# Probability spreads issued in pieces of two copies, and copies of product banks to G on ScalarE or VectorE

## The chip, the cores and the metric

The kernel runs on one core of a Trainium2 chip. A core has five engines with queues of their own: TensorE (PE in the profile; its weight loads are PEld), VectorE (DVE), ScalarE (ACT), GpSimd (POOL) and SyncE (SP, which here issues DMAs only). Each engine takes its instructions in the order in which the program lists them, and waits for others by semaphores. Matrix products land in PSUM banks of 128 x 512 fp32, which only TensorE, ScalarE and VectorE reach in this kernel; everything else lies in SBUF or in DRAM.

The metric is the device time of one execution in microseconds, smaller is better.

## The reference

Sparse attention over 8 batches and 8 heads, then a feed-forward layer with a gated activation:

```python
def _attn_ref(q, k, v):                      # (8, 8, 576, 64) fp32
    ...
    rel = pos[:, None] - pos[None, :]
    mask_local = (rel >= 0) & (rel < 32)
    mask_strided = (rel >= 0) & (pos[None, :] % 32 == pos[:, None] % 32)
    # heads 0 to 3 use mask_local, heads 4 to 7 mask_strided
    ...
    attn = np.exp(scores)
    attn = attn / (np.sum(attn, axis=-1, keepdims=True) + 1e-09)
    return np.matmul(attn, v)

def _moe_ref(x, w_in, w_out):                # x: (4608, 512), d_ff = 2048
    h = x @ w_in
    g = h * np.clip(h + 3.0, 0.0, 6.0) / 6.0
    return g @ w_out
```

## The kernel before

**Attention** goes by pairs of heads (`pair(g)`, four pairs to a batch, two local and two strided). For each head of a pair the scores lie in a tile `e`. VectorE, ScalarE and GpSimd turn them into probabilities (mask, maximum, exponential, sum, division). For batches 2 to 7 VectorE then transposes them in place in 32 x 32 blocks (`flip`, L691), and ScalarE copies the blocks to their places in a larger tile `at`, which is zero elsewhere (`spread`, L693 to L701): a local head takes six copies of 32 partitions (L701, tile `atloc`), a strided head four (L698, tile `atstr`). All copies of one head are one operation of the plan. In a strided pair GpSimd then sets a column of `e` again (`again`, L704), and TensorE multiplies `at` with the values (`values`, L725; matmuls in L400 and L736).

**The feed-forward layer** works on tiles of 512 tokens. Every fp32 operand is split into a high and a low part, and every product takes three matmuls (high x high, high x low, low x high). Batches 0, 1 and 2 go through plain tiles (`ffn`). Batches 3 and 4, then 5 and 6, then 7 with the remaining rows of all batches, go in three double tiles, which use Strassen's scheme: seven products P1 to P7 in place of eight for a 2 x 2 block of hidden units (`product`, matmuls in L1130 to L1132, six for each product). The first double tile is `super_tile`, the two others are `fast_tile`; `form` prepares their operands (`B_B`, `B_T`, splits in L1060 and L1064, differences in L1070).

The products of a step share two PSUM banks, `("ph", 0)` and `("ph", 1)`. P1, P6, P7 and P4 use the one, P2, P5 and P3 the other. Some products begin a bank anew, others add to what the bank holds, since the scheme needs running sums. After a product its bank has to be read before the next product may write there. It is read in one of three ways:

- `copied` (L1135): the bank is copied into a tile `G` (or `r`) in SBUF by ScalarE, L1137. Three of the seven products of a step are read so: 72 copies in the whole kernel, 24 in each double tile.
- `added` (L1140): VectorE adds the bank to what `G` holds, L1142. The gate follows on it: a Relu by ScalarE (L777) and a product by VectorE (L780).
- for P4 the gate reads the bank itself (L1334 and L1338 in `fast_tile`).

In `fast_tile` the second layer is a product with seven terms as well (matmuls in L1453 to L1455, read by VectorE in L1465 to L1471); its operands are sums of the G tiles (L1402 to L1411) and their splits (L1364 and L1368).

**The order of the work** comes from a planner in the kernel, `Plan`. Each call of `op` gives an engine (or several, in a dictionary with the time for each), an estimated time in us, what it reads and writes, and a due time. `emit` walks forward in time like a simulator. For each engine it looks for the operation that can start first, and among equals for the one due first; then it takes the engine whose first operation starts earliest. The engines are looked at in the order in which their names first occur in the plan, and a later one is taken only if it is strictly earlier:

```python
for e, r in ready.items():
    ...
    if first is not None and (best is None or first[0] < best[0]):
        best = (first[0], e, first[2])
```

GpSimd and VectorE occur ahead of ScalarE. An operation that follows another on the same engine is available 0.02 us after it (L154). When all is placed, the instructions are issued in the order of the planned starts; on the chip each engine keeps that order, whatever the real times are.

The function that holds L693 to L706 is `pair`; `copied` stands in L1135 to L1138.

Of the kernel before, what the change touches and what calls it, by code (L numbers as in the profile page):

```python
# [28 lines left out]
PAD = 32  # L29
# [31 lines left out]
class Plan:  # L61
# [12 lines left out]
    def op(self, engine, us, fn, reads=(), writes=(), due=0.0, room=0.0, mode="", after=0.0, take=None, give=None, early=0.0):  # L74
        n = len(self.ops)
        before = set()
        for k in reads:
            if k in self.wrote:
                before.add(self.wrote[k])
            self.used.setdefault(k, []).append(n)  # L80
        for k in writes:
            if k in self.wrote:
                before.add(self.wrote[k])
            before.update(self.used.pop(k, ()))
            self.wrote[k] = n
        before.discard(n)
        how = engine if isinstance(engine, dict) else {engine: us}
        self.ops.append((how, fn, before, due, room, mode, after, take, give, early))
        return n
# [85 lines left out]
def attention_ffn(ctx: ExitStack, tc, q, k, v, w_in, w_out, out):  # L175
    nc = tc.nc
# [21 lines left out]
    op = plan.op  # L198
    tiles = {}
# [121 lines left out]
    def slot(early):  # L321

        return Slot([("acc", i) for i in range(4 if early == 2 else 2)] + [("s", i) for i in range(2)] if early else [("s", i) for i in range(2)])

    def psum(key, name):
        return new(pp, key.key if isinstance(key, Slot) else key, [P, TOK], F32, name)
# [17 lines left out]
    def timing(g):  # L344
        b = g // NPAIR
        if not b:
            return T0 - 6.0 * (NPAIR - g)
        return wanted[b] - 6.0 - (NPAIR - 1 - g % NPAIR) * (wanted[b] - opens[b]) / NPAIR
# [20 lines left out]
    def upright(ps, half, c0, data):  # L369

        rows = data.shape[0]
        nc.tensor.matmul(ps[D * half:D * half + D, c0:c0 + rows], data, tiles["ident",][:rows, :rows], start=True, stop=True)
# [68 lines left out]
    def pair(g):  # L441
# [3 lines left out]
        loc = h0 < H // 2  # L445
        nm = f"{b}_{c}"
        early = (b == 0) + (g == 0)
        due = timing(g)
# [30 lines left out]
        for x in "qk":  # L479
# [6 lines left out]
            if early:  # L486
# [32 lines left out]
                for h in range(2):  # L519
                    op({"ACT": 0.45, "DVE": 0.4} if loc else {"ACT": 0.65, "DVE": 0.65}, 0, partial(evac, h=h), reads=[tb[h]],  # L520
                       writes=[tkey[x]] if h == 0 else [(tkey[x], 1)], give=tb[h], due=due - 19)
# [49 lines left out]
        ekeys = [("el" if loc else "es", j) for j in range(2)]  # L571
        akeys = [("at64" if first else "atl" if loc else "at", j) for j in range(2)]
        stkey = ("st", g % 2)
        nblk = NQB if loc else 8
        n = QB if loc else P
# [4 lines left out]
        def e_whole(j):  # L580
            t = tiles["e", j]
            return t[:QB, :NQB * WIN].rearrange("p (u x) -> p u x", x=WIN) if loc else \
                t[:, NQB * WIN:NQB * WIN + 8 * PAD].rearrange("p (u x) -> p u x", x=PAD)
# [30 lines left out]
        for j in range(2):  # L614
# [5 lines left out]
            def keep(j=j):  # L620
# [17 lines left out]
               writes=[ek, st], give=banks[j], due=sd + 0.5)  # L638
# [40 lines left out]
        for j in range(2):  # L679
            def turn(j=j):  # L680
                at, e = tiles[akeys[j]], e_whole(j)
                for a in range(n // PAD):
                    rows = slice(PAD * a, PAD * a + PAD)
                    if not loc:
                        nc.vector.transpose(at[rows, :, rows], e[rows])
                        continue
                    for h in range(2):
                        nc.vector.transpose(at[PAD * (a + h):PAD * (a + h) + PAD, :, rows], e[rows, :, PAD * h:PAD * h + PAD])
            if b >= 2:
                def flip(j=j):  # L690
                    nc.vector.transpose(e_whole(j)[:, :, :2 * PAD if loc else PAD], e_whole(j)[:, :, :2 * PAD if loc else PAD])  # L691

                def spread(j=j):  # L693
                    at, e = tiles[akeys[j]], e_whole(j)
                    for a in range(n // PAD):
                        rows = slice(PAD * a, PAD * a + PAD)
                        if not loc:
                            nc.scalar.copy(at[rows, :, rows], e[rows])  # L698
                            continue
                        for h in range(2):  # L700
                            nc.scalar.copy(at[PAD * (a + h):PAD * (a + h) + PAD, :, rows], e[rows, :, PAD * h:PAD * h + PAD])  # L701

                def again(j=j):
                    nc.gpsimd.memset(e_whole(j)[:, :, NPOS:NPOS + 1], 1.0e-9)  # L704
                op("DVE", 0.55 if loc else 0.4, flip, writes=[ekeys[j]], due=due - 2 + j)
                op("ACT", 6 * 0.31 if loc else 4 * 0.36, spread, reads=[ekeys[j]], writes=[akeys[j]], due=due - 1.9 + j)  # L706
                if not loc:
                    op("POOL", 0.15, again, writes=[ekeys[j]], due=due - 1.8 + j)
                continue
            if not first:  # L710
                op("DVE", 6 * 0.37 if loc else 4 * 0.435, turn, reads=[ekeys[j]], writes=[akeys[j]], due=due - 2 + j)
                continue
            tb = slot(early)

            def stand(j=j, tb=tb):
                ps = psum(tb, f"pe{nm}{j}")
                for i in range(NQB):
                    upright(ps, i // 3, i % 3 * QB, e_whole(j)[:, i, :w])

            def copy(j=j, tb=tb):  # L720
                nc.scalar.copy(tiles["at64"][:, j], tiles[tb.key][:, :3 * QB])
            op("PE", 0.7 * slow, stand, reads=[("ident",), ekeys[j]], writes=[tb], take=tb, due=due - 1002 + j, mode="s")
            op("ACT", 0.45, copy, reads=[tb], writes=[akeys[j]], give=tb, due=due - 2 + j)
# [409 lines left out]
        op("PE", 1.367, mm, reads=[("wr", wn)] + [bkey(si, bn, k) for k in range(2)], writes=[pk], due=due, mode="f")  # L1133

    def copied(to, writes, pk, due):  # L1135
        def go():
            nc.scalar.copy(to(), tiles[pk])  # L1137
        op("ACT", 0.6, go, reads=[pk], writes=writes, due=due)  # L1138

    def added(to, key, pk, due):  # L1140
        def go():
# [33 lines left out]
    def super_tile(si):  # L1175
# [45 lines left out]
        for n in range(NFC // 2 + 1):  # L1221
# [10 lines left out]
            for x in sorted(TURN, key=lambda x: isinstance(x, str)):  # L1232
# [13 lines left out]
                if x == "P1":  # L1246
                    copied(lambda rk=rk, nm=nm: new(xp, rk, [P, TOK], F32, f"r{nm}"), [rk], pc, du)
                elif x == "P2":
                    r_of = lambda rk=rk: tiles[rk]
                    added(r_of, rk, pa, du)  # L1250
                    gate_ops(rk, us[0], du, f"u{nm}a", r_of, pa)
                    split_ops(gks[0], r_of, rk, du, f"{nm}a")
                elif x == "P6":
                    copied(partial(g_of, n0, True), g_first(n0), pc, du)
                elif x == "P7":
                    copied(partial(g_of, n1, True), g_first(n1), pc, du)
                elif x == "P5":
                    to = partial(g_of, n1, False)
                    added(to, g_key(n1), pa, du)
                    gate_ops(g_key(n1), us[1], du, f"u{nm}b", to)  # L1260
                elif x == "P4":
                    gate_ops(pc, us[2], du, f"u{nm}c")
                    split_ops(gks[1], lambda u=us[2]: tiles[u], us[2], du, f"{nm}c")
                else:
                    to = partial(g_of, n0, False)
                    added(to, g_key(n0), pa, du)
                    gate_ops(g_key(n0), us[3], du, f"u{nm}d", to, pa)
# [266 lines left out]
    for g in range(NPAIR):  # L1534
        pair(g)
# [9 lines left out]
    for g in range(NPAIR, 4 * NPAIR):  # L1545
        pair(g)
    keep_plain()
    ffn(1)
    for g in range(4 * NPAIR, 5 * NPAIR):
        pair(g)  # L1550
# [54 lines left out]
```

## Time and profile before

| what | value |
|---|---|
| median of 3 runs | 871.46 us (869.53 to 873.02) |
| the profiled execution's own time | 870.54 us |
| its span, first to last instruction | 868.8 us |
| mean granted TensorE clock | 0.991 |
| spread copies, local (L701) | 144, 50.8 us in all |
| spread copies, strided (L698) | 96, 38.6 us in all |
| bank copies (L1137) | 64 to G and 8 to r, 37.5 and 4.7 us in all |

How to read it: the profile shows one execution. Rows of groups give the source line, the engine, the operation, output and input tiles by their names, and the count. A wait is put down to the engine whose work came last. Idle time of an engine is a loss only where the end of the kernel hangs on it. TensorE's busy time counts overlapping matmuls once, and says nothing of how fast each one ran.

### The profile page before, as it was taken

To read this page: it belongs to the slowest core of one execution; us is meant where nothing else is said; L and a number is where in the kernel's file an instruction comes from. 1 tells how busy PE (TensorE), PEld (TensorE's weight loads), DVE (VectorE), ACT (ScalarE), POOL (GpSimd) and SP (SyncE) were. 2 spreads that over 40 slices of the span, in tenths; PEclk is the share of its full clock that TensorE was granted. 3 is DMA by queue.
4 is the path that set the end of the run, shared out by engine and by line. 5 is a ranking of instruction groups with operands and counts; after the bars stand their busy time and mean duration, and the time that the engine had idled before them with its cause. 6 is when DMAs were issued, how large, how long until landed. Compare 5 with 4: busy or idle time off the path is not lost.

```text
span 868.8 us, 18930 instructions
## 1 busy us (share of the span) xinstructions
PE 846.6 (97%) x6954; PEld 683.0 (79%) x6954; DVE 537.6 (62%) x898; ACT 557.9 (64%) x1246; POOL 615.3 (71%) x606
## 2 busy tenths in 40 slices
PE   8899999999999999999999999999999999999996
PEld 7577778788888788888888888788888778888884
DVE  6588878344454538454546664566767888555586
ACT  4587657678778866877677955776744645454441
POOL 5488876687547799767676994465974987767573
PEclk9899999999999999999999999999999999999998
DMA  8978713798974455899999898876566667866536
GB/s 199 313 158 240 231 30 83 205 290 237 295 216 116 119 129 159 219 268 250 243 285 287 272 314 212 230 206 197 180 203 188 190 179 223 243 195 194 182 122 145
DMA packets 323308, 179.12 MB, mean 206 GB/s; under 512 B 182864, under 2 KB 300368, under 8 KB 323216
## 3 DMA queue, kind: packets, MB, share of 16 engines
q1 hardware_dynamic: 318564, 176.27, 71.8%
q10 hardware_dynamic: 4652, 1.64, 0.9%
q8 instruction: 55, 0.90, 0.4%
q14 instruction: 37, 0.30, 0.1%
HBM read 136.97 MB, written 40.89 MB: 205 GB/s over the span
## 4 chain that ended last, share of the span: by engine, by line
PE 87%; POOL 5%; DVE 4%; ACT 2%; issue 2%; POOLq 0%; DVEq 0%; ACTq 0%
PE P L1130 8%; PE P L1131 8%; PE P L1132 8%; PE cP L1453 5%; PE cP L1454 5%; PE cP L1455 5%; PE acc L834 5%; PE ph L857 5%; PE ph L858 4%; PE ph L859 4%; PE acc L835 4%; PE acc L836 4%; PE acc L1215 4%; PE acc L1217 3%; PE acc L1216 3%; PE pv L736 2%
## 5 line engine op out<-in xcount | busy, mean ns | idle before, releaser
L1471 DVE SCALAR_TENSOR_TENSOR C<-cP,C 128x512 f32<-128x512 f32 x96 | 65.7, 687 | 40.5 <-PE cP L1455 39.8
L795 POOL TENSOR_TENSOR gl<-u,gh 128x512 fp32r<-128x512 f32 x48 | 65.2, 1360 | 34.1 <-ACT gh L791 17.9
L1142 DVE TENSOR_TENSOR G<-P,G 128x512 f32<-128x512 f32 x64 | 44.0, 689 | 65.1 <-PE P L1132 52.7
L1130 PE MATMUL P<-B_T,wr 128*128 128x512 f32 x192 | 76.1, 397 | 3.9 <-ACT G L1137 2.3
L834 PE MATMUL acc<-wo,gh 128*128 128x512 f32 x192 | 77.3, 403 | 0.0
L836 PE MATMUL acc<-wo,gl 128*128 128x512 f32 x192 | 75.2, 392 | 0.3 <-POOL gl L795 0.2
L835 PE MATMUL acc<-wo,gh 128*128 128x512 f32 x192 | 75.1, 391 | 0.0
L1131 PE MATMUL P<-B_T,wr 128*128 128x512 f32 x192 | 74.9, 390 | 0.0
L1132 PE MATMUL P<-B_T,wr 128*128 128x512 f32 x192 | 74.9, 390 | 0.0
L1137 ACT COPY G<-P 128x512 f32<-128x512 f32 x64 | 37.5, 586 | 52.3 <-PE P L1132 51.9
L1368 POOL TENSOR_TENSOR sp<-G,sp 128x512 fp32r<-128x512 f32 x34 | 47.5, 1408 | 24.8 <-ACT sp L1364 22.6
L666 POOL TENSOR_TENSOR e<-e,st 128x144 f32<-128x144 f32 (+1 forms) x64 | 44.2, 693 | 18.8 <-DVE st L662 15.7
L780 DVE SCALAR_TENSOR_TENSOR u<-u,ph 128x512 f32<-128x512 f32 x48 | 32.8, 684 | 38.2 <-ACT u L777 38.1
L857 PE MATMUL ph<-x,wi 128*128 128x512 f32 x128 | 52.6, 411 | 2.3 <-ACT x L427 1.2
L701 ACT COPY atloc<-e 32x192 f32<-32x192 f32 x144 | 50.8, 353 | 2.5 <-DVE e L691 1.1
L858 PE MATMUL ph<-x,wi 128*128 128x512 f32 x128 | 51.0, 398 | 0.6 <-DVE x L430 0.5
L859 PE MATMUL ph<-x,wi 128*128 128x512 f32 x128 | 50.8, 397 | 0.0
L777 ACT ACTIVATE u<-ph,three 128x512 f32<-128x512 f32 x48 | 33.0, 687 | 27.2 <-PE ph L859 26.9
L1130 PE MATMUL P<-B_B,wr 128*128 128x512 f32 x120 | 47.1, 393 | 0.0
L1131 PE MATMUL P<-B_B,wr 128*128 128x512 f32 x120 | 46.8, 390 | 0.0
L1130 PEld LDWEIGHTS P<-B_T,wr 128*128 128x128 f32 x192 | 36.1, 188 | 13.7 <-ACT G L1137 3.6
L1132 PE MATMUL P<-B_B,wr 128*128 128x512 f32 x120 | 46.8, 390 | 0.0
(604 smaller groups left out, 2648.1 us busy)
## 6 DMA issues: line engine op xcount, KB each, us to landing
wr<-dA SPq DMA_DIRECT2D x72, 256.0 KB
or<-do SPq DMA_DIRECT2D x32, 512.0 KB
wr<-dSu SPq DMA_DIRECT2D x48, 256.0 KB
wr<-dSv SPq DMA_DIRECT2D x48, 256.0 KB
or<-do SPq DMA_DIRECT2D x48, 256.0 KB
rawi<-in_moe_w_in_dram SPq DMA_DIRECT2D x16, 512.0 KB
rawo<-in_moe_w_out_dram SPq DMA_DIRECT2D x16, 512.0 KB
do<-wo SPq DMA_DIRECT2D x16, 512.0 KB
```

Source lines behind the costliest of these rows:

```text
L701: nc.scalar.copy(at[PAD * (a + h):PAD * (a + h) + PAD, :, rows], e[rows, :, PAD * h:PAD * h + PAD])
L795: (nc.vector if tail else nc.gpsimd).tensor_tensor(out=to, in0=src(), in1=tiles[gk[0]].bitcast(F32), op=ALU.subtract)
L834: nc.tensor.matmul(acc, gh, woh, start=fc == 0, stop=False)
L835: nc.tensor.matmul(acc, gh, wol, start=False, stop=False)
L836: nc.tensor.matmul(acc, gl, woh, start=False, stop=end)
L857: nc.tensor.matmul(ph, wih, xh, start=n_ == 0, stop=False)
L858: nc.tensor.matmul(ph, wih, xl, start=False, stop=False)
L859: nc.tensor.matmul(ph, wil, xh, start=False, stop=n_ == NCC - 1)
L1130: nc.tensor.matmul(ph, wh, xh, start=fresh and k == 0, stop=False, skip_group_check=not fresh)
L1131: nc.tensor.matmul(ph, wh, xl, start=False, stop=False, skip_group_check=not fresh)
L1132: nc.tensor.matmul(ph, wl, xh, start=False, stop=k == 1, skip_group_check=not fresh)
L1471: nc.vector.scalar_tensor_tensor(out=tiles[ck], in0=tiles[bank], scalar=1.0 / 6.0, in1=tiles[ck], op0=ALU.mult, op1=ALU.add)
```

## The change

A spread is no longer one operation of the plan but three (local head) or two (strided head), each of two copies. The copies are the same, in the same order, on ScalarE. Each piece reads and writes the same tiles as the whole did, so one follows another; other operations of ScalarE may come between them. The planned times add up to the same sum as before (1.86 and 1.44 us).

A bank copy may go to ScalarE (0.6 us planned) or to VectorE (0.68 us planned); the planner takes the engine on which it can start first.

```diff
-                def spread(j=j):
+                def spread(part, j=j):
                     at, e = tiles[akeys[j]], e_whole(j)
-                    for a in range(n // PAD):
+                    for a in part:
                         rows = slice(PAD * a, PAD * a + PAD)
                         if not loc:
                             nc.scalar.copy(at[rows, :, rows], e[rows])
...
-                op("ACT", 6 * 0.31 if loc else 4 * 0.36, spread, reads=[ekeys[j]], writes=[akeys[j]], due=due - 1.9 + j)
+                parts_ = ((0,), (1,), (2,)) if loc else ((0, 1), (2, 3))
+                for i, part in enumerate(parts_):
+                    op("ACT", 0.31 * 2 if loc else 0.36 * 2, partial(spread, part), reads=[ekeys[j]], writes=[akeys[j]], due=due - 1.9 + j)
...
     def copied(to, writes, pk, due):
-        def go():
-            nc.scalar.copy(to(), tiles[pk])
-        op("ACT", 0.6, go, reads=[pk], writes=writes, due=due)
+        def go(e):
+            if e == "ACT":
+                nc.scalar.copy(to(), tiles[pk])
+            else:
+                nc.vector.tensor_copy(to(), tiles[pk])
+        op({"ACT": 0.6, "DVE": 0.68}, 0, go, reads=[pk], writes=writes, due=due)
```

## The prediction

> **What bounds the kernel now.** I read the page first: busy times, and the chain that ended last.
>
> ```profile
> span 868.8 us, 18930 instructions
> PE 846.6 (97%) x6954; PEld 683.0 (79%) x6954; DVE 537.6 (62%) x898; ACT 557.9 (64%) x1246; POOL 615.3 (71%) x606
> PE 87%; POOL 5%; DVE 4%; ACT 2%; issue 2%; POOLq 0%; DVEq 0%; ACTq 0%
> ```
>
> TensorE is busy for 97% of the span, and the chain runs on it for 87%. The change takes nothing off TensorE, so it can only win back time in which TensorE stands still, and only after the first changed instruction. When that is, and what it costs, the answers for one line each show (count, then shortest/median/longest in ns, then first and last start in us).
>
> ```profile
> L701 ACT COPY atloc<-e x144: 336/353/362, 149.4 to 590.1; 32x192 f32<-32x192 f32 x144
> L698 ACT COPY atstr<-e x96: 385/402/409, 170.8 to 621.8; 32x256 f32<-32x256 f32 x96
> L1137 ACT COPY G<-P x64: 577/587/591, 356.8 to 830.4; 128x512 f32<-128x512 f32 x64
> L1137 ACT COPY r<-P x8: 563/587/591, 350.7 to 470.9; 128x512 f32<-128x512 f32 x8
> ```
>
> So the spreads (L701, L698) begin at 149.4 us and the bank copies (L1137, 64 + 8 = 72 of them) end at 831 us. The planner walks forward in time, so what lies ahead of 149 us stays as it is. I then cut the rest into stages: the view of stretches gives, for each, its length and the busy time of PE, PEld, DVE, ACT and POOL, with the granted clock, the DMA share and GB/s behind.
>
> ```profile
> 145.00:350.00 205.00, 205.00 (x1962) 165.39 (x1961) 103.66 (x196) 153.90 (x409) 147.83 (x168) 1.00 0.69 194
> 350.00:545.00 195.00, 195.00 (x1574) 158.79 (x1573) 104.04 (x172) 139.34 (x335) 140.52 (x146) 1.00 0.93 258
> 545.00:565.00 20.00, 18.36 (x138) 14.24 (x136) 11.31 (x21) 15.17 (x34) 10.95 (x14) 1.00 0.90 252
> 565.00:670.00 105.00, 104.98 (x662) 86.06 (x662) 73.04 (x105) 64.97 (x135) 72.56 (x60) 1.00 0.67 195
> 670.00:708.00 38.00, 35.66 (x155) 28.55 (x154) 33.39 (x38) 21.09 (x36) 34.73 (x24) 1.00 0.58 177
> 708.00:845.00 137.00, 137.00 (x604) 112.97 (x603) 88.08 (x123) 66.95 (x110) 92.82 (x68) 1.00 0.65 194
> ```
>
> TensorE is full in four of the six. It idles 20 - 18.36 = 1.64 us between 545 and 565, where the first fast tile starts, and 38 - 35.66 = 2.34 us between 670 and 708, where the last one starts: 3.98 us in all, plus 0.02. That is everything the change can win, 0.46% of the time. The list of waits names the releasers (total us, times, longest).
>
> ```profile
> ACT G L1137 <- PE P L1132: 51.9, 45, 2.9
> PE P L1130 <- ACT G L1137: 2.3, 3, 1.0
> PE P L1130 <- DVE G L1142: 1.6, 1, 1.6
> ```
>
> Three stalls, 2.3 us together, end with a bank copy, and one of 1.6 us with an addition on VectorE. Yet the first row says that ScalarE itself sat idle before 45 of the 64 copies to G until TensorE had finished the product: most copies start at once and can't come sooner on any engine.
>
> **The change part by part.**
>
> *The three stalls behind a copy.* The timeline at 553, 560 and 690 us (start, duration, what; in brackets the idle time before):
>
> ```profile
> 553.02 0.39 PE L1132 MATMUL P<-B_B,wr 128*128 128x512 f32 x1
> 553.42 0.69 DVE L1338 SCALAR_TENSOR_TENSOR G<-G,P 128x512 f32<-128x512 f32 x1
> 553.45 0.58 ACT L1137 COPY G<-P 128x512 f32<-128x512 f32 x1
> 554.09 0.50 PE L1130 MATMUL P<-B_T,wr 128*128 128x512 f32 x1 [0.68 <-ACT G L1137]
> ...
> 558.50 1.63 ACT L698 COPY atstr<-e 32x256 f32<-32x256 f32 x4
> 558.63 1.10 DVE L780 SCALAR_TENSOR_TENSOR G<-u_1P,G 128x512 f32<-128x512 f32 x1
> 559.44 0.39 PE L1132 MATMUL P<-B_T,wr 128*128 128x512 f32 x1
> 560.15 0.58 ACT L1137 COPY G<-P 128x512 f32<-128x512 f32 x1
> 560.79 0.50 PE L1130 MATMUL P<-B_T,wr 128*128 128x512 f32 x1 [0.96 <-ACT G L1137]
> ...
> 690.14 0.40 PE L1132 MATMUL P<-soonB,wr 128*128 128x512 f32 x1
> 690.17 1.54 DVE L1064 TENSOR_TENSOR B_T<-tk,B_T 128x512 fp32r<-128x512 f32 x1
> 690.57 0.58 ACT L1137 COPY G<-P 128x512 f32<-128x512 f32 x1 [0.43 <-PE P L1132]
> 691.21 0.50 PE L1130 MATMUL P<-B_T,wr 128*128 128x512 f32 x1 [0.67 <-ACT G L1137]
> ```
>
> At 553 the product ends at 553.02 + 0.39 = 553.41 and the copy starts at 553.45: nothing to win. VectorE is in L1338 until 554.11, so it would only be later. At 690 it is the same: product end 690.54, copy 690.57, VectorE busy until 691.71. At 560 the copy is late: the product ends at 559.83 and ScalarE is in a spread until 560.13, so 560.15 - 559.83 = 0.32 us is lost to the uncut spread. Cut after its second copy, at 559.31, the product isn't there yet, and the second piece would start; but VectorE is free from 559.73. A copy there would start at about 559.87 (the 0.04 us of the other two) and end 0.69 later at 560.56, against 560.73 now. Worth -0.2 us; with a fitting order on ScalarE up to -0.3. I take -0.2.
>
> What the copy costs on VectorE the trace doesn't show for this very operation. The nearest row is VectorE's other evacuation of a 128x512 bank with one operand:
>
> ```profile
> L1467 DVE TENSOR_SCALAR C<-cP x5: 692/692/692, 578.6 to 747.0; 128x512 f32<-128x512 f32 x5
> ```
>
> I take 692 ns, that is 105 ns more than ScalarE's 587, since this reader of a bank keeps its time to the nanosecond in five places. The bound above is 1.77 us, if the copy were drawn out like the SBUF operation L1405 at 698.79 (quoted below); the bound below is 587 ns, no difference. Where no TensorE wait hangs on the copy, the 105 ns are hidden: TensorE works on another bank for one product of six matmuls.
>
> *How many copies move.* When both engines are free, the planner looks at VectorE first and ScalarE must be strictly earlier, so a tie goes to VectorE. The view of stretches, asked for L1137 alone (length, ScalarE's busy time and count; the last two of five rows), gives the copies of each stage: 27, 3, 15, 6 and 21.
>
> ```profile
> 670.00:708.00 38.00, 3.53 (x6) 1.00 0.58 177
> 708.00:845.00 137.00, 12.33 (x21) 1.00 0.65 194
> ```
>
> Estimated with VectorE's idle share of each stage, from the rows above: 27 x 47% + 3 x 43% + 15 x 30% + 6 x 12% + 21 x 36% = 27 copies. That adds 27 x 0.692 = 18.7 us to VectorE and takes 15.8 us off ScalarE, both beside a full TensorE: 0 on the path. If all 72 moved VectorE would have 49.8 us more, still short of full in each long stage (708 to 845: 88.1 + 21 x 0.692 = 102.6 of 137).
>
> *The stall of 1.6 us.* First VectorE's timeline at the stall, then the chain of waits (start, length, work) where GpSimd's unbroken run begins that leads to it:
>
> ```profile
> 697.11 1.76 DVE L1408 TENSOR_TENSOR S<-G,G 128x512 f32<-128x512 f32 x1 [0.81 <-POOL G L1402]
> 698.79 1.77 DVE L1405 TENSOR_TENSOR G<-G,G 128x512 f32<-128x512 f32 x1
> 700.49 1.28 DVE L1142 TENSOR_TENSOR G<-P,G 128x512 f32<-128x512 f32 x2
> ```
>
> ```profile
> 696.96 0.59 ACT L1137 COPY G<-P 128x512 f32<-128x512 f32 x1 [2.90 <-PE P L1132]
> ```
>
> ```profile
> 672.82 0.59 ACT G L1137
> 673.40 0.53 ACT B_T L1060
> 674.00 1.02 POOL B_T L1064
> ```
>
> VectorE has two drawn-out operations (1.76 and 1.77 us) ahead of the addition that TensorE waits for, and a wait for GpSimd ahead of those. Two copies touch this. The one at 696.96 finds ScalarE idle for 2.90 us and VectorE idle too (the 0.81 us before 697.11): a tie, so it goes to VectorE, ends at 697.65 and holds L1408 back from 697.11: +0.54 us on the stall; if it stays, 0. The one at 672.82 stands on ScalarE ahead of the cast L1060 that lets GpSimd begin. If it moves, the cast can start up to one copy earlier (-0.59 us, for the whole run of GpSimd behind it); if it stays, 0. I take +0.5 and -0.5, both copies moved: 0.
>
> *The spreads in pieces.* The same 144 + 96 copies, no instruction more. A piece is available 0.02 us after the one before, and the planner starts what can start first, so at each cut any ready operation of ScalarE goes ahead, pressing or not. Between 149 and 545 TensorE has no idle time that earlier gates could fill, so the gain there is 0, hidden by TensorE's own queue. What it costs: the products with values and GpSimd's memset (L704) wait for the last piece; TensorE waits for no spread today, and the planner puts the product at its new time. I take 0.
>
> Sum: -0.2 + 0.5 - 0.5 = **-0.2 us**. The profiled execution took 870.54 us (its span and 1.7 us around it), 0.9 below the median of 871.46; on the median the forecast is **871.3 us**, no change that can be measured.
>
> **The rivals.**
>
> *The stalls go.* The new order might let TensorE find work in both transitions: 871.46 - 3.98 = 867.5 us. For it: ScalarE is busy for 76% of the first transition (15.17 of 20) and 55% of the second (21.09 of 38), so there is room to reorder. Against: 45 of 64 copies already start at once, and the two banks stay two. Chance 0.20.
>
> *VectorE's queue takes the place of ScalarE (slower).* Between 670 and 708 VectorE is busy 33.39 of 38 us (88%), ScalarE 21.09 (55%). All six copies there on VectorE are 6 x 0.692 = 4.15 us more for an engine with 4.61 us idle, and the rows above have it without a gap from 697.11 to 701.8, so nearly all of it lands on the stall: 875.6 us; with one more drawn-out operation (1.78 - 0.69 = 1.09) 876.7. It decides from four moved copies on (+2.8 us). Against: at 690.57 VectorE is busy until 691.71, and the planner then takes ScalarE. The Trainium skill speaks for this rival: Perfetto Trace Analysis, "Optimizing Scalar/DVE Operations", advises to offload to ScalarE where VectorE is saturated, and this change goes the other way; the trace's 88% against 55% in this stage agrees, the rest of the kernel doesn't. Chance 0.17.
>
> *The pieces make the attention late.* Two cuts in a local spread, at each up to one group of six exponentials (6 x 0.336 = 2.0 us by the row below): 4.0 us later in all; where the plan misjudges this by more than its room of 1.2 us, TensorE stands for 2.8 us, and two such waits give 877.1 us.
>
> ```profile
> L656 ACT ACTIVATE e<-e,st 96x64 f32<-96x64 f32 x144 | 36.7, 336 | 4.3 <-DVE st L645 4.2
> ```
>
> Against: the planner itself orders those exponentials and so knows the delay. Chance 0.08.
>
> The same section of the Trainium skill says that breaking up instructions may help where an engine that isn't saturated causes bubbles on others. By that rule the cut gains; the trace has one such bubble behind a spread, the 0.32 us at 560, so the sum would be 871.46 - 0.3 = 871.2.
>
> *The copies stay on ScalarE* because it is free too: 871.5 us. Chance 0.05.
>
> **How the numbers follow.** The forecast has 0.50, the rivals 0.20, 0.17, 0.08 and 0.05. About 0.5% (4.4 us) is what a measurement of this kernel tells from no change. The first rival falls short of it by a hair at its full size, and the runs before scatter over 3.5 us, so 0.12 of its 0.20 count as faster. Of the second 0.11 and of the third 0.07 pass the bound: slower 0.18. The rest, 0.70, is the same. The range goes from all stalls gone (867.5) to the six copies on VectorE (875.6), each with 0.5 us for scatter: 867.0 to 876.1.
>
> **What would show it.** Right: TensorE without idle time from 145 to 545 and from 708 to 845; the copies split over two engines, VectorE's near 0.69 us; idle time of TensorE at the two transitions between 2 and 6 us in all; pairs of spread copies with a gate or copy between them. Wrong: TensorE idle in a steady stage, waits of TensorE for a spread or for an addition queued behind a copy, copies on VectorE above 0.8 us, or both transitions closed.

## The result, and the profile after

The changed kernel takes 876.10 us (median of 6 runs, 874.70 to 878.48), the kernel before 869.04 (6 runs beside them). The ratio is 1.0069 [1.0044, 1.0095]: slower, by 6.0 us, with the interval from 3.8 to 8.3 us. (The two medians lie 7.1 us apart; the 6.0 us are the ratio's.) The forecast was 871.3 us and no measurable change. The profiled execution took 875.71 us.

The page's head, then the stretches that the prediction cut (length; busy time of PE, PEld, DVE, ACT and POOL; granted clock, DMA share, GB/s):

```profile
span 873.9 us, 18936 instructions
PE 850.0 (97%) x6954; PEld 686.3 (79%) x6954; DVE 567.3 (65%) x939; ACT 541.1 (62%) x1206; POOL 613.5 (70%) x605
```

```profile
350.00:545.00 195.00, 190.02 (x1516) 153.68 (x1515) 115.97 (x187) 130.70 (x314) 139.78 (x147) 0.98 0.90 251
545.00:565.00 20.00, 19.53 (x167) 15.58 (x166) 9.71 (x14) 11.75 (x28) 6.32 (x7) 1.00 0.81 230
565.00:670.00 105.00, 105.00 (x664) 86.19 (x663) 79.47 (x124) 62.13 (x134) 71.12 (x63) 1.00 0.69 198
670.00:708.00 38.00, 35.74 (x156) 28.94 (x155) 32.08 (x38) 21.59 (x37) 32.20 (x23) 1.00 0.64 196
708.00:845.00 137.00, 136.91 (x601) 112.52 (x600) 96.62 (x131) 59.94 (x98) 92.72 (x68) 1.00 0.65 192
```

Where TensorE had no idle time at all, from 350 to 545, it now has 195 - 190.02 = 4.98 us of it, and the granted clock of that stage is 0.98. The first transition got better, 0.47 us idle against 1.64; the second is as it was, 2.26 against 2.34. The list of waits (total us, times, longest) names the releaser, and the timelines of TensorE, VectorE and GpSimd (start, length, work; in brackets the idle time before) show the place:

```profile
PE P L1132 <- DVE G L1147: 5.6, 2, 4.1
PE P L1132 <- DVE u_4c L782: 0.7, 1, 0.7
```

```profile
483.32 0.39 PE L1222 MATMUL acc<-or,gl_6c 128*128 128x512 f32 x1
487.77 0.79 PE L1132 MATMUL P<-B_B,wr 128*128 128x512 f32 x1 [4.06 <-DVE G L1147]
488.36 0.63 PE L1133 MATMUL P<-B_B,wr 128*128 128x512 f32 x1
488.78 0.63 PE L1134 MATMUL P<-B_B,wr 128*128 128x512 f32 x1
```

```profile
477.81 0.65 DVE L1066 TENSOR_TENSOR B_B<-x,B_B 128x512 fp32r<-128x512 f32 x1
479.18 0.58 DVE L691 STREAM_TRANSPOSE e<-e 96x384 f32<-96x384 f32 x1 [0.72 <-POOL e L666]
479.69 7.42 DVE L1066 TENSOR_TENSOR B_B<-x,B_B 128x512 fp32r<-128x512 f32 x1
487.03 0.68 DVE L1147 TENSOR_TENSOR G<-P,G 128x512 f32<-128x512 f32 x1
```

```profile
479.11 1.29 POOL L1173 TENSOR_TENSOR sp<-sp,sp 128x512 fp32r<-128x512 f32 x1
480.36 1.28 POOL L797 TENSOR_TENSOR gl_7a<-r,gh_7a 128x512 fp32r<-128x512 f32 x1
481.61 1.28 POOL L1173 TENSOR_TENSOR sp<-sp,sp 128x512 fp32r<-128x512 f32 x1
482.86 1.26 POOL L797 TENSOR_TENSOR gl_2e<-G,gh_2e 128x512 fp32r<-128x512 f32 x1
484.09 2.47 POOL L1157 TENSOR_TENSOR sp<-or 128x512 f32<-128x512 f32 x2
```

Read the four together. The same operation on VectorE, a low part with both operands in SBUF (L1066), takes 0.65 us at 477.81 and 7.42 us at 479.69. GpSimd runs six operations without a gap from 479.11 to 484.09 + 2.47 = 486.56 (they end a longer run that began at 473.58), and VectorE's operation ends 0.55 us after the last of them, at 487.11. The addition that empties TensorE's bank (L1147) is queued behind it and comes at 487.03. TensorE has by then nothing left that it may do.

The wait is not the whole price. The matmuls after it start 0.59, 0.42 and then 0.43 us apart, where matmuls of this size otherwise start 0.23 us apart. Two stretches show the clock (columns as above):

```profile
483.00:487.70 4.70, 0.71 (x4) 0.24 (x2) 4.70 (x3) 0.00 (x0) 3.56 (x3) 0.87 0.76 237
487.70:491.00 3.30, 3.23 (x8) 2.56 (x9) 2.51 (x5) 3.16 (x8) 0.00 (x0) 0.50 0.02 5
```

It is 0.50 after the wait. Adding up, from 480 to 494, what the starts of TensorE's instructions lie beyond 0.227 us apart (only distances over 0.25 us) gives 7.0 us after and 0.4 us before, so this one place costs 6.6 us. Of the 7.0 us the wait is 4.2 and the slow starts behind it, until 493.4, are 2.7. The Trainium skill, TensorE: Matmul & The Clock Gate, "Part 1: The HAM clock gate", says that the clock halves after an idle window of about 3.4 us and comes back after as long a busy one; the trace agrees in kind and not in the times. Its clock record has 0.50 from 486.49 to 493.32 us and 1.00 on both sides. So the clock fell 2.8 us after the last matmul had ended (483.71) and came back 5.6 us after the matmuls had begun again (487.77).

To see whether anything else grew, I took the start of the k-th matmul with 512 columns from both traces. The first is at 38.69 us before and 38.53 after, the 1350th at 407.87 and 407.19, the 1800th at 523.08 and 529.50, the 3150th at 844.90 and 850.68, and the spans end at 868.75 and 873.92. So the changed kernel is 0.7 us ahead at 407 us, 6.4 us behind at 523, and regains 1.3 us by the end. All the loss arises in one stage, and nearly all in one place of it.

The copies did what the change says. By line (lowest, median and highest ns; first and last start in us):

```profile
L1140 ACT COPY G<-P x30: 567/589/590, 355.1 to 833.4; 128x512 f32<-128x512 f32 x30
L1140 ACT COPY r<-P x2: 587/588/590, 369.0 to 418.9; 128x512 f32<-128x512 f32 x2
L1142 DVE COPY G<-P x34: 672/692/693, 361.5 to 836.1; 128x512 f32<-128x512 f32 x34
L1142 DVE COPY r<-P x6: 690/692/692, 348.6 to 472.2; 128x512 f32<-128x512 f32 x6
```

40 of the 72 moved, at a median of 692 ns. The last one on VectorE ahead of the wait starts at 475.58, four microseconds before the long operation.

### The profile page after: what moved, and what is told of

Same layout as the page of the kernel before. It is cut to its first block, busy times and chain, and to the rows that moved or that the text cites. A ratio compares the mean times of both kernels' runs of the same rounds, so it can differ in the third digit from the quotient of the medians.

```text
span 873.9 us, 18936 instructions
## 1 busy us (share of the span) xinstructions
PE 850.0 (97%) x6954; PEld 686.3 (79%) x6954; DVE 567.3 (65%) x939; ACT 541.1 (62%) x1206; POOL 613.5 (70%) x605
## 3 DMA queue, kind: packets, MB, share of 16 engines
q10 hardware_dynamic: 4652, 1.64, 0.8%
## 4 chain that ended last, share of the span: by engine, by line
PE 79%; POOL 6%; DMA 5%; DVE 4%; issue 2%; ACT 2%; SPq 0%; POOLq 0%; DVEq 0%; ACTq 0%
PE P L1132 8%; PE P L1134 8%; PE P L1133 8%; PE cP L1458 5%; PE cP L1460 5%; PE cP L1459 5%; PE acc L836 5%; PE ph L859 5%; PE acc L838 4%; PE acc L837 4%; PE ph L861 4%; PE ph L860 4%; PE acc L1220 3%; PE acc L1221 3%; PE acc L1222 3%
## 5 line engine op out<-in xcount | busy, mean ns | idle before, releaser
L666 POOL TENSOR_TENSOR e<-e,st 96x384 f32<-96x384 f32 (+1 forms) x64 | 45.5, 713 | 23.4 <-DVE st L662 22.1
L1147 DVE TENSOR_TENSOR G<-P,G 128x512 f32<-128x512 f32 x64 | 43.9, 687 | 24.9 <-PE P L1134 24.1
L859 PE MATMUL ph<-x,wi 128*128 128x512 f32 x128 | 51.9, 406 | 2.3 <-ACT x L427 1.2
L782 DVE SCALAR_TENSOR_TENSOR u<-u,ph 128x512 f32<-128x512 f32 x48 | 32.7, 682 | 33.0 <-ACT u L779 32.9
L1132 PE MATMUL P<-B_B,wr 128*128 128x512 f32 x120 | 48.0, 400 | 5.2 <-DVE G L1147 4.1
L860 PE MATMUL ph<-x,wi 128*128 128x512 f32 x128 | 50.2, 392 | 1.2 <-DVE x L430 1.2
L659 DVE TENSOR_REDUCE st<-e 96x6 f32<-96x390 f32 (+1 forms) x64 | 27.1, 428 | 37.3 <-ACT e L653 19.3
L861 PE MATMUL ph<-x,wi 128*128 128x512 f32 x128 | 50.2, 392 | 0.5 <-POOL wi L309 0.5
L645 DVE TENSOR_REDUCE st<-e 96x6 f32<-96x384 f32 (+1 forms) x64 | 26.0, 415 | 33.2 <-POOL e L641 32.9
L1133 PE MATMUL P<-B_B,wr 128*128 128x512 f32 x120 | 47.3, 394 | 0.0
L1134 PE MATMUL P<-B_B,wr 128*128 128x512 f32 x120 | 47.2, 394 | 0.0
```

The source lines that it names most:

```text
L859: nc.tensor.matmul(ph, wih, xh, start=n_ == 0, stop=False)
L860: nc.tensor.matmul(ph, wih, xl, start=False, stop=False)
L861: nc.tensor.matmul(ph, wil, xh, start=False, stop=n_ == NCC - 1)
L1132: nc.tensor.matmul(ph, wh, xh, start=fresh and k == 0, stop=False, skip_group_check=not fresh)
L1133: nc.tensor.matmul(ph, wh, xl, start=False, stop=False, skip_group_check=not fresh)
L1134: nc.tensor.matmul(ph, wl, xh, start=False, stop=k == 1, skip_group_check=not fresh)
```

## The experiments

Three theories were on record. **Lock-out**: the new order, whatever made it new, lets the low part on VectorE meet GpSimd's gapless run with the addition behind it. **Copies**: 40 copies more on VectorE make it late. **Pieces**: the cut spreads make the attention late.

**Each half alone** (the two parts of the diff above, one at a time).

> Only the spreads are cut into pieces; the bank copies stay on ScalarE. Lock-out theory (a VectorE operation with two SBUF operands doesn't get in between GpSimd operations that follow one another without a gap, and an addition queued behind it holds TensorE): the pieces cost nothing by themselves; the time is that of before, 869 to 871, unless the new order happens to put such an operation ahead of an addition, and then the trace shows a VectorE operation of over 3 us and a TensorE wait for L1142's addition of 2 us or more. Copies theory (each copy moved to VectorE loads its queue): 869 to 870, since no copy moves. Pieces theory (the attention comes late): about 876, with TensorE waiting at products with values.

> Only the bank copies may go to VectorE; the spreads stay whole. Lock-out theory: some 40 copies move at no cost; 867 to 871 unless the order happens to lock an operation out ahead of an addition (a VectorE operation over 3 us in the trace, and then 873 to 877). Copies theory: about 876, as the whole change, with TensorE's waits spread over the double tiles. Pieces theory: 869 to 870.

The pieces alone: 869.56 us, ratio 0.9981 [0.9961, 1.0001]. The copies alone: 869.05 us, ratio 0.9978 [0.9958, 0.9998]. Neither half is slow, so neither their load nor their cuts is what costs. In both traces no VectorE operation after 100 us lasts over 2 us. The stages from 350 to 545 and to 565 us, of the pieces alone and then of the copies alone:

```profile
350.00:545.00 195.00, 194.73 (x1572) 158.30 (x1571) 105.53 (x178) 143.89 (x345) 141.13 (x147) 1.00 0.95 262
545.00:565.00 20.00, 19.53 (x144) 15.45 (x143) 10.47 (x17) 13.14 (x27) 8.96 (x11) 1.00 0.80 226
```

```profile
350.00:545.00 195.00, 195.00 (x1574) 158.74 (x1573) 111.27 (x187) 131.65 (x320) 143.21 (x148) 1.00 0.94 259
545.00:565.00 20.00, 18.54 (x139) 14.53 (x138) 13.25 (x24) 14.90 (x33) 10.65 (x14) 1.00 0.91 246
```

TensorE is full again, or nearly so (194.73 of 195), and the clock 1.00. The copies and pieces theories fall as loads. What is left is the order that the two make together.

**The one operation on GpSimd**, everything else in the changed kernel's order (operation 2454 of the plan is the low part at 479.69):

```diff
-                ops[n][1](e)
+                ops[n][1]("POOL" if n == 2454 else e)
```

> The changed kernel with its order kept, but the one VectorE operation that took 7.42 us (the low part of an operand, L1066, at 479.7 us) is issued on GpSimd at the same place. Lock-out theory: the TensorE wait of 4.06 us at 483 us goes, the slow matmuls behind it (427 ns apart instead of 227, 13 of them) go with it, and the time falls by 4.1 + 2.6 = 6.7 us to 869 to 870, though GpSimd gets 1.3 us more to do just there. Copies theory and pieces theory: all copies and pieces are where they were, so no more than 1 us changes, 875 to 876.

871.64 us, ratio 1.0004 [0.9987, 1.0022]. The wait at 483 is gone. The lock-out isn't: the next two-operand operation of VectorE met the same run of GpSimd.

```profile
484.82 5.64 DVE L782 SCALAR_TENSOR_TENSOR G<-u_7b,G 128x512 f32<-128x512 f32 x1 [0.57 <-ACT u_7b L779]
490.39 0.67 DVE L782 SCALAR_TENSOR_TENSOR u_7c<-u_7c,P 128x512 f32<-128x512 f32 x1
```

VectorE is held for 5.64 us, but no addition that TensorE needs at once is behind, and TensorE waits only 1.0 us nearby (`PE ps L601 <- ACT x L427`). So it isn't the long operation that costs the time, but what is queued behind it.

**A gap in GpSimd's run**: a copy of one column, put behind GpSimd's L1173, that waits for VectorE's operation.

```diff
-                ops[n][1](e)
+                ops[n][1](e); behind() if n == 2454 else None
...
-        plan.emit(idle)
+        plan.emit(idle, lambda: nc.gpsimd.tensor_copy(pause, operand(1, "B21", 1)[:, 1, :1].bitcast(F32)))
```

> The changed kernel with that operation still on VectorE and every queue's order kept, but GpSimd gets one more instruction behind its operation L1173 at 479.1 us: a copy of one column of the result, so that it waits for VectorE's operation and leaves it a gap. Lock-out theory: VectorE's operation shrinks from 7.42 to 1.3 to 2.0 us, GpSimd loses about 1 us there, TensorE's wait of 4.06 us goes, and the time falls to 869 to 870. If the 7.42 us came from something else than GpSimd's unbroken run (a semaphore, an operand not yet there), the operation stays over 7 us and the time at 876 or above.

876.04 us (869.27 to 879.32), ratio 1.0047 [1.0023, 1.0072]: the time did not come back. The runs fall into two groups: three took 869.3 to 870.2 us and nine 874.9 to 879.3. The traced one (876.72) is of the second. GpSimd's timeline and the waits of TensorE:

```profile
483.20 1.29 POOL L1173 TENSOR_TENSOR sp<-sp,sp 128x512 fp32r<-128x512 f32 x1
485.11 0.19 POOL L1579 COPY pause<-B_B 128x1 f32<-128x1 f32 x1 [0.61 <-DVE B_B L1066]
```

```profile
PE P L1132 <- DVE G L782: 1.4, 1, 1.4
PE acc L1220 <- DMA or<-do: 1.2, 1, 1.2
PE acc L1220 <- ACT B_T L1062: 0.6, 1, 0.6
```

VectorE's operation took 1.26 us and the wait at 483 is gone, as the lock-out theory has it. But GpSimd's sums of the `or` slots (L1157), which free them for their next loads, end at 492.01 instead of 486.56. Of these 5.45 us, 3.7 are the later start of this execution (below) and 1.8 the gap. Three waits that the changed kernel has not, or has only for 0.2 us, take 3.2 us. Against the traced execution of the kernel before, this one is 6.2 us longer: 3.5 of them lie ahead of TensorE's first 512-column matmul, 2.1 between the 1350th and the 1800th, where the changed kernel loses 7.1, and 0.8 behind, less 0.2 gained ahead of it. So the loss at the wait is mostly gone in the trace. Whether the eight other slow runs also lose their time at the start isn't recorded, so the result on the time is inconclusive: the run shows that the gap frees VectorE, and that holding GpSimd up brings waits of its own.

**One move in VectorE's queue alone.** `moved` takes one operation out of the plan's list and puts it ahead of another (0) or behind it (1); all other queues are as in the changed kernel. The low part goes ahead of the transpose that stood before it, or behind the addition that stood after it; the third kernel also swaps two gates at 431 us, where a lesser wait (0.7 us) has the same cause.

```diff
-        for _, _, n, e in sorted(order):
+        for _, _, n, e in moved(sorted(order), 2454, 2405, 0):   # e5: ahead of the flip L691
...
+        for _, _, n, e in moved(sorted(order), 2454, 2029, 1):   # e6: behind the addition L1147
...
+        for _, _, n, e in moved(moved(sorted(order), 2454, 2405, 0), 1869, 1872, 1):   # e7: e5, and gate u_4c ahead of u_4b
```

> The changed kernel with one exchange in VectorE's queue and every other queue as it was: the operand's low part (L1066) is issued ahead of the transpose (L691) at 479.2 us instead of behind it, so that it begins before GpSimd's run of six operations. Nothing is added to GpSimd. Lock-out theory: the operation takes 2 us or less instead of 7.42, TensorE's wait of 4.06 us at 483 us and the slow matmuls behind it go; the 6.7 us come back but for what the next waits there take (the run with the gap showed about 3.5 us of them, when GpSimd was held up; here it is held up 0.5 us at most): 869 to 872. Copies theory and pieces theory: nothing of theirs is touched, 875 to 877.

> The changed kernel with the opposite exchange: the low part (L1066) is issued behind the addition (L1147) that held TensorE. Lock-out theory: the addition starts as soon as its product is done, at about 482.4 us, so TensorE's wait at 483 us goes; the low part then meets the rest of GpSimd's run and takes up to 3.5 us (until 486.6), and the transpose and the gates behind it are late by that, so 0 to 3 us of new TensorE waits: 869 to 873. If TensorE's wait hung on something else than the queue behind the locked-out operation, it stays at 4 us and the time at 876.

> As the exchange ahead, and a second one: at 431 us the gate that reads a bank (u_4c) is issued ahead of the gate with both operands in SBUF (u_4b), which took 3.19 us beside three GpSimd operations and held TensorE for 0.71 us at 435 us. Lock-out theory: that wait goes too, 0.7 to 0.9 us below the run with one exchange, 868 to 871, at or below the time of before. Copies theory and pieces theory: 875 to 877.

Ahead: 872.00 us, ratio 1.0009 [0.9987, 1.0031]. Behind: 870.81 us, 0.9998 [0.9982, 1.0013]. With the gates: 871.11 us, 0.9994 [0.9975, 1.0013]. By these runs each gives the 0.7% back. In the first and the third the gate behind is kept out in its turn (L782 at 485.12 and 484.50, 5.00 us each), with nothing behind it that TensorE needs at once, as when the low part went to GpSimd. The second is the sharpest, since it leaves the lock-out in place. Its VectorE:

```profile
479.54 0.69 DVE L1147 TENSOR_TENSOR G<-P,G 128x512 f32<-128x512 f32 x1 [0.65 <-PE P L1134]
480.14 6.18 DVE L1066 TENSOR_TENSOR B_B<-x,B_B 128x512 fp32r<-128x512 f32 x1
486.24 1.21 DVE L534 STREAM_TRANSPOSE qplain<-qn 128x576 f32<-128x576 f32 x1
```

The same operation is still kept out, for 6.18 us, until GpSimd's run ends; only the addition now stands ahead of it, and TensorE's longest wait from 350 to 545 us is 1.5 us instead of 4.1. The cause of the 0.7% is shown by these: an addition queued behind an operation that GpSimd keeps out. Only the run with the gap, where that wait went and the time stayed, doesn't fit as it stands.

A look at the traces alone says how complete this is. From the 1350th to the 1800th matmul with 512 columns the kernel before takes 115.2 us, the changed one 122.3, the halves 114.5 (pieces) and 115.1 (copies). With the low part on GpSimd it is 116.7, with the gap 117.3, ahead 117.2, behind 118.8, and with the gates 115.3. Every repair shortens the stretch, and in these single executions other waits keep up to half of the 7.1 us (behind: 1.5 us for a load, 1.4 for ScalarE). The verdict on the time rests on the runs, twelve of each.

**Why is it kept out so long?** In three kernels all computation was left out but short runs of GpSimd subtractions, with one VectorE operation started beside them.

```diff
+        nc.scalar.copy(a, src)
+        for i in range(many):
+            nc.gpsimd.tensor_tensor(out=spots[i], in0=a, in1=b, op=ALU.subtract)
+        if cols:
+            nc.vector.transpose(before[:, :cols], a[:, :cols])
+        if what == "two":
+            nc.vector.tensor_tensor(out=two, in0=a, in1=b, op=ALU.subtract)
...
```

> The disputed wait by itself; all of the computation is left out and the output is zeros. In each stage ScalarE writes a tile, then GpSimd subtracts from it 0 to 8 times in a row without a gap, and VectorE does a transpose of 32 to 512 columns (to vary when it comes) and one operation: with two operands in SBUF, with one in a bank and one in SBUF, or a copy of a bank. Lock-out theory: the operation with two SBUF operands takes 0.7 us beside no GpSimd operation and in some stages waits over two and more of GpSimd's operations, up to the length of the run (8 x 1.3 us); the operations that read a bank take 0.69 us in every stage. If VectorE always gets in at the first boundary, no operation takes over 2 us, and the 7.42 us have another cause.

The groups of the first of the three (count, then busy us and mean ns; `two` has both operands in SBUF, `one` one of two in PSUM, `bank` is a copy from PSUM), then one stage of its timeline:

```profile
L45 DVE TENSOR_TENSOR two<-start,other 128x512 f32<-128x512 f32 x18 | 25.9, 1438 | 0.0
...
L49 DVE COPY bank<-ps 128x512 f32<-128x512 f32 x3 | 2.0, 654 | 0.0
L47 DVE TENSOR_TENSOR one<-ps,start 128x512 f32<-128x512 f32 x3 | 2.0, 653 | 0.0
```

```profile
85.15 10.25 POOL L41 TENSOR_TENSOR pool<-start,other 128x512 f32<-128x512 f32 x8 [0.73 <-ACT start L39]
85.54 1.42 DVE L45 TENSOR_TENSOR two<-start,other 128x512 f32<-128x512 f32 x1
```

An operation with an operand in PSUM is not touched by GpSimd (653 ns beside eight of its operations). One with two in SBUF ends at 85.54 + 1.42 = 86.96, that is 1.81 us after GpSimd's start, whether two or eight GpSimd operations run: it gets in at the first boundary, and GpSimd's next operation is drawn out from 1.26 to 1.71 us instead. So the length of the run isn't the reason.

> All computation is left out; the output is zeros. 95 stages, each with four GpSimd subtractions back to back and one VectorE subtraction with both operands in SBUF, which VectorE reaches after a transpose and one or two copies of a PSUM bank cut so that it starts in steps of about 8 to 17 ns from 0.2 to 1.3 us after GpSimd's first one. In the previous experiment, at 0.09 to 0.59 us, it always got in at the first boundary (end at 1.81 us, GpSimd's second one drawn out from 1.22 to 1.67 us). Theory A, the moment decides: in the kernel's traces the operations that were kept out to the end of GpSimd's run had begun 0.56 to 0.66 us after the start of the GpSimd operation in progress; so stages that begin there end at about 4 x 1.22 + 0.55 = 5.4 us instead of 1.81. Theory B, the moment doesn't decide and something else in the kernel's instructions does: every stage that begins before about 1.1 us ends at 1.81 us, and those within 0.1 us ahead of the boundary or behind it end at about 3.0 us, one boundary later.

> All computation is left out; the output is zeros. Ten kinds of stage at four moments each (about 0.25, 0.5, 0.55 and 0.95 us after GpSimd's start), each with six GpSimd operations back to back and one two-operand VectorE operation: plain; GpSimd's results rounded to fp32r; VectorE's result rounded; VectorE on tiles of its own; VectorE in place; GpSimd in place; GpSimd behind roundings of ScalarE, as the low parts are; a mix; sums of a tile's two halves; operands that a DMA has just brought. Theory A (the moment decides): the same moments in every kind are kept out, for about 6 x 1.22 us. Theory B (the kind of instruction decides): in one or several kinds VectorE's operation takes 5 to 7 us, at all four moments, and in the others it ends at the first boundary, 1.81 us after GpSimd's start. Theory C (neither): all forty end at the first boundary or, at the last moment, at the second, and what keeps VectorE out in the kernel stays open.

The moment isn't either: over 95 stages the operation got in at the boundary that it found next, unless it began in the last 0.05 us of the GpSimd operation in progress (lowest, median and highest ns):

```profile
L45 DVE TENSOR_TENSOR two<-start,other x95: 681/1355/1802, 3.6 to 577.7; 128x512 f32<-128x512 f32 x95
```

Nor is it any of the ten kinds (rounded results, operations in place, GpSimd behind ScalarE's roundings, sums of a tile's halves, operands just loaded): the longest took 1.73 us.

```profile
L77 DVE TENSOR_TENSOR two<-start,other x24: 682/1251/1732, 15.6 to 322.9; 128x512 f32<-128x512 f32 x24
L81 DVE TENSOR_TENSOR vlow<-vone,vtwo x8: 714/1250/1729, 77.1 to 260.7; 128x512 fp32r<-128x512 f32 x8
```

One of the forty began after its GpSimd run and tells nothing. From the 22nd on, VectorE's operation came beside the run of the stage before, in its midst. The 39 began 0.08 to 1.10 us after the start of the GpSimd operation in progress, and each got in at that operation's end. The lock-out over several operations appears only inside the full kernel, and why GpSimd goes first at those boundaries and VectorE at most others **stays open**.

## Why the prediction was wrong

**The step that failed** is the one that priced whatever lies beside a full TensorE at nothing: "Between 149 and 545 TensorE has no idle time that earlier gates could fill, so the gain there is 0", and of the moved copies "both beside a full TensorE: 0 on the path". The row behind it (195.00 of 195.00 us busy) says that the additions came in time in the order of before. It says nothing of a new order. A new order has no more work, but other neighbours, and here one new neighbourhood cost 6.6 us. The prediction summed engine time and did not ask which VectorE operations with two SBUF operands would now begin beside a long run of GpSimd with an addition behind them.

**The cover that it named was too thin.** The copies were said to be hidden because "TensorE works on another bank for one product of six matmuls". That is about 6 x 0.23 = 1.4 us of cover (TensorE did have more work at 479, until 483.7), against an operation of 7.42 us. The longest VectorE operations that the prediction quoted were 1.76 and 1.77 us, so its bound from above for one meeting with GpSimd was four times too low. The trace of the kernel before had a longer one, which the prediction does not show. It too ends 0.55 us after a run of GpSimd (484.93), in the stage that was priced at nothing:

```profile
482.87 2.61 DVE L780 SCALAR_TENSOR_TENSOR G<-u_7b,G 128x512 f32<-128x512 f32 x1
```

**The rival with the right sign had the wrong mechanism.** "VectorE's queue takes the place of ScalarE" gave 875.6 us, and the time is 876.10. But its place was 670 to 708 us and its price the copies themselves. There one copy of six moved, not the four from which it decides, and TensorE's idle time there is 2.26 us, as before. It is VectorE's queue, but not the copies in it, and at another place: the agreement in microseconds is chance. "The pieces make the attention late" had its place in the right stage, but no wait for a spread is in the list.

**What held.** The copy on VectorE was put at 692 ns and measured 692. The estimate of 27 moved copies was low (40): from 350 to 545 us alone VectorE has 15 of them, against 9 on ScalarE.

**What came out right by luck.** The second transition was forecast unchanged, as +0.5 and -0.5 for "both copies moved", and is unchanged. The two copies that these terms hang on (672.82 and 696.96 us before) stayed on ScalarE, the second of them although the prediction counted it as a tie that VectorE wins. So both terms were 0, and only their sum was right:

```profile
678.58 0.59 ACT L1140 COPY G<-P 128x512 f32<-128x512 f32 x1 [0.57 <-PE P L1134]
702.72 0.59 ACT L1140 COPY G<-P 128x512 f32<-128x512 f32 x1 [2.90 <-PE P L1134]
```

The first transition was to gain 0.2 us by a copy on VectorE, and gained 1.64 - 0.47 = 1.17, while its three copies stayed on ScalarE (561.69, 564.56 and 565.86). The rows of the halves alone (shown with the first experiment) have 0.47 us idle there for the pieces and 1.46 for the copies, so it was the pieces: that term was six times too small and had the wrong way to its gain.

**The signs.** The first sign that the prediction listed as wrong, "TensorE idle in a steady stage, waits of TensorE for a spread or for an addition queued behind a copy", is nearly what came; the operation ahead of the addition is a low part, not a copy.

**Is there a version that beats both?** The copies alone, 0.9978 [0.9958, 0.9998], is the only one whose interval lies below 1, and by a fifth of a per cent. With seven versions measured, one interval that ends this close to 1 is weak evidence.

## What to carry to other kernels

A full TensorE in the profile is a property of an order, not of a stage: before a change that lets a planner reorder is priced at nothing, list the operations of VectorE with two SBUF operands, and see what would be late if one of them had to wait for GpSimd's whole run. Put what TensorE needs next ahead of such an operation; here one move in one queue was worth 0.7%. And take the two halves of a change apart on the chip, because two harmless halves can make a harmful order.

## What the runs showed of the hardware

**GpSimd can keep VectorE out over several of its operations.** Five of the kernels here have an operation of VectorE that took 5.0 to 7.4 us beside a gapless run of GpSimd, always ending 0.55 us after the run's end. The end of the run isn't needed: the gate u_4b (L782) took 3.19 us in the changed kernel, from 431.45, and got in at GpSimd's third boundary (434.07) while the run went on to 436.01. Four other traces have it so at the same place, with 3.16 to 3.19 us. This is rare. Six of the traces (before, after, and the first four experiments) have 822 VectorE operations of 128x512 with two SBUF operands. Of these, 608 began while a GpSimd operation (memsets aside) was in progress: 24 got in at once, 561 at the first boundary, 18 at the second and 5 later. The Trainium skill, SBUF — State Buffer, "SBUF: two separate sides", says that the two share a port pair as an exclusive lock, held for a whole instruction, where a VectorE operation with two SBUF inputs meets a GpSimd operation that reads SBUF; the first small kernel agrees (PSUM operand 653 ns, two SBUF operands 1.2 to 1.7 us). That VectorE may lose at three to five boundaries in a row is seen only in the full kernels.

**A wait of TensorE of 4.06 us cost more than itself**: eleven matmuls started 0.43 us apart, and with the slower starts at both ends of them that is 2.7 us. The wait of 1.6 us at the second transition, which every version has, is followed by starts 0.22 to 0.24 us apart again after one of 0.34.

**The start varies.** Up to TensorE's first 512-column matmul all the full kernels run the same program, and yet it starts at 37.85 us in one traced execution and at 42.20 in another. One trace of each kernel would therefore mislead by several microseconds if only the spans were compared.
